# An mLSTM and a squared-ReLU feed-forward in one kernel: a new hand-written order of its 1,280 steps

## The chip, the cores and the metric

The kernel runs on one core of one Trainium2 chip. Its metric is the time of one execution on the device, in microseconds. Five engines work side by side, each through its own list of instructions in order: TensorE (PE, with its weight loads PEld), VectorE (DVE), ScalarE (ACT), GpSimd (POOL) and SyncE (SP), which here issues all DMAs. An engine waits for another by semaphores.

## The reference

The first part is a gated recurrence (mLSTM) per batch and head, with B = 4, H = 8, S = 768 and D = 40; the second is a token-shift feed-forward over the 320 joined channels, with 1,024 hidden ones.

```python
for t in range(S):
    m_new = np.maximum(f_gate[:, :, t] + m, i_gate[:, :, t])
    f_stab = np.exp(f_gate[:, :, t] + m - m_new)
    i_stab = np.exp(i_gate[:, :, t] - m_new)
    C = f_stab * C + i_stab * outer(vt, kt)
    n = f_stab * n + i_stab * kt
    h_tilde = C @ qt
    y[:, :, t] = sigmoid(o_gate[:, :, t]) * h_tilde / np.maximum(np.abs(n @ qt), 1.0)
x_prev = shift(x)                       # x is y with the heads side by side
xk = mu_k * x + (1 - mu_k) * x_prev
xr = mu_r * x + (1 - mu_r) * x_prev
k = np.maximum(xk @ w_k, 0.0)
out = sigmoid(xr @ w_r) * ((k * k) @ w_v)
```

## The kernel before

The sequence is cut into 6 chunks of 128 tokens. Two batches with the same chunk make one unit, so there are 12 units `u`, each with two halves `i`. Inside a chunk the recurrence is computed as a masked attention; between chunks a state `C` per batch is carried.

A unit's first stage goes: `load_s` brings k and q (`kq`, two loads of 320 KB, to 40 partitions each), `load_v` v and k in token order, `load_o` the output gates; `fetch_m` spreads the running maxima over all partitions and `mask` (GpSimd) makes them causal; `exps` (ScalarE) takes the exponentials; `scores` (TensorE, tile `pS`) and `weigh` (VectorE, writes `e`) give the weights; `attend` (TensorE, tiles `pI` and `pX`) the sums; `norm`, `gate`, `outcome` and `twin` scale them to `x`; `turn` (TensorE) and `turned` (ScalarE) transpose. For unit 0 there is no earlier `fetch_m`, and `spread` makes the maxima by matmuls into `pM`.

The second stage: `change` makes x minus x_prev, `mix` (VectorE, three instructions of 128x256 for each of k and r) the mixed input `xm`. fp32 products are made from parts: each operand is split into a high part (`mix_h`, ScalarE, tile `xh`) and a low part (`mix_l`, tile `xl`), and three products of parts are summed. `ffn_k` (tile `pk`), `relu`, `square`, `square_h` (`kh`) and `square_l` (`kl`) give the hidden layer in four groups, `ffn_v` (tile `pv`) the second product, `ffn_r` (tile `pr`) the gate, `result` and `store` the output.

The weights are loaded by the kernel itself as 64-bit words (`load_w`) and turned into fp32 and then into parts on the chip: `size` (ScalarE), three `bits` steps (VectorE), `parts` (ScalarE, the high part) and `parts_l` (the low part: `wkl`, `wvl`), for three of them by a `differ` on TensorE. There are 8 pieces of wk, 8 of wv and 3 of wr. `stack` copies rows of wk and wr by DMA. `warm(n)` issues n matmuls on an identity, whose result is not used.

Each engine's program is set by the list of calls at the end of the kernel: the scheduler is switched off (`manual_schedule`), and a call appends its instructions to the engines they belong to. Some calls name their engine, `V`, `G` (GpSimd), `A` or `SY` (SyncE). So the list alone decides what stands behind what on every engine and in SyncE's DMA queue. The list has 1,283 calls, from the line `every = ExitStack()` on. Semaphores order what depends on each other across engines. SyncE issues at most eight DMAs ahead: the ninth waits for the landing of the first.

Of the kernel before, what the change touches and what calls it, by code (L numbers as in the profile page):

```python
# [39 lines left out]
def mlstm_cmix_kernel(ctx: ExitStack, tc, kq, vk, og, gi, gf, wk, wr, wq, wv, mu, pad, out):  # L40
# [519 lines left out]
    load_w("wk", 0, SY)  # L560
    warm(4)
    begin()
    load_w("wk", 7, SY)
    warm(4)
    size("wk", 0)
    size("wk", 7)
    warm(4)
    load_w("wk", 6, SY)
    gate_b(0)
    warm(4)  # L570
    gate_m(0)
    load_w("wk", 2, SY)
    scale_a(0, V)
    gate_o(0, SY)
    warm(8)
    bits("wk", 0, 0)
    scale_k(0, V)
    warm(4)
    load_w("wk", 1, SY)
    load_s(0, SY)  # L580
    gate_r(0)
    gate_b(1)
    bits("wk", 0, 1)
    bits("wk", 0, 2)
    triangle()
    size("wk", 2)
    zero_state(0, G)
    size("wk", 6)
    bits("wk", 7, 0)
    load_w("wk", 5, SY)  # L590
    parts("wk", 0)
    size("wk", 1)
    bits("wk", 7, 1)
    bits("wk", 7, 2)
    bits("wk", 2, 0)
    load_w("wk", 4, SY)
    bits("wk", 1, 0)
    bits("wk", 6, 0)
    bits("wk", 2, 1)
    parts("wk", 7)  # L600
    load_w("wv", 1, SY)
    bits("wk", 1, 1)
    bits("wk", 2, 2)
    gate_i(1, V)
    zero_state(1, G)
    columns(0)
    spread(0, 0)
    exps(0, 0, 0, 4)
    load_v(0, SY)
    bits("wk", 1, 2)  # L610
    bits("wk", 6, 1)
    parts_l("wk", 0, V)
    load_o(0, SY)
    scores(0, 0)
    parts_l("wk", 7, V)
    load_w("wr", 0, SY)
    exps(0, 0, 4, 8)
    parts("wk", 2)
    bits("wk", 6, 2)
    gate_m(1)  # L620
    size("wk", 4)
    spread(0, 1)
    bits("wk", 4, 0)
    weigh(0, 0, 0)
    size("wv", 1)
    parts_l("wk", 2, V)
    bits("wk", 4, 1)
    scale_a(1, V)
    bits("wv", 1, 0)
    parts("wk", 6)  # L630
    parts("wk", 1)
    load_w("wv", 0, SY)
    gate_o(1, SY)
    scale_d(1, V)
    size("wk", 5)
    bits("wv", 1, 1)
    scale_k(1, V)
    load_w("wk", 3, SY)
    carry_in(0, 0, V)
    weigh(0, 0, 1)  # L640
    exps(0, 1, 0, 4)
    load_o(1, SY)
    gate_r(1)
    bits("wk", 5, 0)
    scores(0, 1)
    gate_b(2)
    bits("wv", 1, 2)
    bits("wk", 4, 2)
    bits("wk", 5, 1)
    gate_i(2, V)  # L650
    parts("wv", 1)
    parts("wk", 4)
    bits("wk", 5, 2)
    load_w("wr", 1, SY)
    fetch_m(1, 0, SY)
    parts_l("wv", 1, V)
    attend(0, 0)
    parts_l("wk", 1, V)
    parts("wk", 5)
    parts_l("wk", 6, V)  # L660
    warm(4)
    norm(0, 0, 0)
    norm(0, 0, 1)
    size("wv", 0)
    zero_state(2, G)
    exps(0, 1, 4, 8)
    load_s(1, SY)
    bits("wv", 0, 0)
    weigh(0, 1, 0)
    warm(4)  # L670
    size("wk", 3)
    fetch_m(1, 1, SY)
    mask(1, 0)
    warm(4)
    load_v(1, SY)
    parts_l("wk", 4, V)
    size("wr", 0)
    differ("wk", 5)
    bits("wr", 0, 0)
    warm(8)  # L680
    bits("wr", 0, 1)
    warm(4)
    norm(0, 0, 2)
    bits("wk", 3, 0)
    carry_in(0, 1, V)
    mask(1, 1)
    sigmoid_o()
    warm(4)
    load_w("wr", 2, SY)
    bits("wr", 0, 2)  # L690
    warm(4)
    bits("wv", 0, 1)
    size("wr", 1)
    parts_l("wk", 5, A)
    zero_state(3, G)
    warm(4)
    carry_add(0, 0)
    gate(0, 0, V)
    scale_a(2, V)
    outcome(0, 0, V)  # L700
    weigh(0, 1, 1)
    load_mu(SY)
    exps(1, 0, 4, 8)
    warm(4)
    bits("wr", 1, 0)
    bits("wr", 1, 1)
    bits("wv", 0, 2)
    stack("wk", 4, 4, 1, SY)
    gate_m(2)
    stack("wk", 4, 4, 0, SY)  # L710
    parts("wr", 0)
    attend(0, 1)
    bits("wk", 3, 1)
    norm(0, 1, 0)
    scores(1, 0)
    twin(0, 0, V)
    exps(1, 0, 0, 4)
    norm(0, 1, 1)
    differ("wr", 0)
    parts("wv", 0)  # L720
    bits("wk", 3, 2)
    carry_add(0, 1)
    norm(0, 1, 2)
    parts("wk", 3)
    gate(0, 1, V)
    bits("wr", 1, 2)
    turn(0, 0)
    warm(8)
    outcome(0, 1, V)
    parts_l("wr", 0, A)  # L730
    differ("wv", 0)
    twin(0, 1, A)
    turned(0, 0)
    weigh(1, 0, 0)
    weigh(1, 0, 1)
    turn(0, 1)
    parts("wr", 1)
    turned(0, 1)
    warm(4)
    parts_l("wk", 3, V)  # L740
    exps(1, 1, 0, 4)
    change(0, 0, V)
    warm(4)
    change(0, 1, V)
    carry_in(1, 0, V)
    warm(4)
    stack("wk", 0, 2, 0, SY)
    exps(1, 1, 4, 8)
    mix(0, "k")
    scores(1, 1)  # L750
    weigh(1, 1, 0)
    mix_h(0, "k")
    attend(1, 0)
    size("wr", 2)
    weigh(1, 1, 1)
    carry_in(1, 1, V)
    warm(8)
    mix_l(0, "k", V)
    bits("wr", 2, 0)
    stack("wk", 0, 2, 1, SY)  # L760
    norm(1, 0, 0)
    warm(4)
    bits("wr", 2, 1)
    norm(1, 0, 1)
    mix(0, "r")
    bits("wr", 2, 2)
    stack("wk", 2, 2, 1, SY)
    parts_l("wv", 0, A)
    norm(1, 0, 2)
    parts("wr", 2)  # L770
    columns(1)
    stack("wk", 2, 2, 0, SY)
    attend(1, 1)
    gate(1, 0, V)
    norm(1, 1, 0)
    parts_l("wr", 1, V)
    load_w("wv", 2, SY)
    outcome(1, 0, V)
    mix_h(0, "r")
    ffn_k(0, 3)  # L780
    carry_add(1, 1)
    stack("wr", 2, 1, 0, SY)
    norm(1, 1, 1)
    relu(0, 3)
    norm(1, 1, 2)
    gate_o(2, SY)
    twin(1, 0, V)
    ffn_k(0, 0)
    parts_l("wr", 2, V)
    mix_l(0, "r", V)  # L790
    stack("wr", 2, 1, 1, SY)
    relu(0, 0)
    turn(1, 0)
    load_w("wv", 3, SY)
    turned(1, 0)
    gate(1, 1, V)
    outcome(1, 1, V)
    scale_d(2, V)
    square(0, 3, A)
    size("wv", 2)  # L800
    load_w("wv", 4, SY)
    twin(1, 1, V)
    ffn_k(0, 1)
    square_h(0, 3, A)
    turn(1, 1)
# [1096 lines left out]
```

## Time and profile before

| | us |
|---|---|
| median of three runs | 332.12 (331.01 to 332.5) |
| the profiled execution's own time | 333.46 |
| its span, first to last instruction | 331.7 |
| TensorE busy / idle in the span | 317.1 / 14.6 |
| VectorE, ScalarE, GpSimd busy | 244.8, 233.1, 108.0 |
| bytes moved by DMA | 43.05 MB, mean 130 GB/s |

The profile is of one execution, whose own time lies 1.76 us over its span. "Busy" of TensorE counts pipelined matmuls; in a row of 128-column warm-ups one takes 0.26 us by its own duration, while they follow each other much faster, so paces are read from the start of one to the start of the next. The clock is the share of full speed that was granted to TensorE.

### The profile page before, as it was taken

The page shows a single profiled execution, that of the slowest core. Times are in us where ns is not written, and L with a number is a line of the kernel's source. Part 1 is how long each engine was busy: PE and PEld are TensorE (multiplying, and loading weights), DVE is VectorE, ACT ScalarE, POOL GpSimd, SP SyncE. Part 2 cuts the span into 40 slices and gives each one's busy share as a digit, 9 for nine tenths or more (in the row PEclk, how much of TensorE's full clock was granted, in tenths as well). Part 3 has the DMA queues.
Part 4 walks back from the last instruction along what each step waited for, and adds up shares of the span by engine and source line. Part 5 has one row for each costly group of instructions (what it writes and reads, how often), then busy time and mean ns, then how long its engine had stood idle before and what let it go on. Part 6 is the DMA issues. An engine that isn't in the chain of part 4 may idle for free.

```text
span 331.7 us, 8880 instructions
## 1 busy us (share of the span) xinstructions
PE 317.1 (96%) x3571; PEld 300.9 (91%) x3571; DVE 244.8 (74%) x548; ACT 233.1 (70%) x508; POOL 108.0 (33%) x128
## 2 busy tenths in 40 slices
PE   5798899989999999999999999999999999999995
PEld 4577699979989999999999999999999999999995
DVE  4698989998898794798698884797956556588111
ACT  3669858999665983936787688668749949855670
POOL 2001100122645613554513425346313157311340
PEclk9557999999999999999999999999999999999999
DMA  6989327946555253332733514536126034010001
GB/s 207 280 274 275 71 59 251 290 153 175 186 176 183 73 128 94 94 119 77 250 105 84 200 67 130 174 105 191 56 85 186 17 92 155 2 42 3 0 22 59
DMA packets 17218, 43.05 MB, mean 130 GB/s; under 512 B 4264, under 2 KB 7912, under 8 KB 16216
## 3 DMA queue, kind: packets, MB, share of 16 engines
q1 hardware_dynamic: 17176, 42.48, 42.0%
q8 instruction: 28, 0.46, 0.6%
q14 instruction: 14, 0.11, 0.1%
HBM read 37.75 MB, written 4.03 MB: 126 GB/s over the span
## 4 chain that ended last, share of the span: by engine, by line
PE 68%; DMA 9%; DVE 8%; issue 5%; ACT 5%; POOL 2%; SPq 1%; POOLq 0%; ACTq 0%
PE pk L492 24%; PE pv L547 19%; PE pI L285 6%; PE pS L255 6%; PE pr L525 6%; DMA sg<-og 4%; DMA kq<-kq 4%; PE pX L291 2%; PE pT L363 2%; ACT e L244 2%; PE pM L233 1%; POOL xlk L396 1%; DMA gi_sb<-gi 1%; PE pX L297 1%; DVE wvl L458 1%
## 5 line engine op out<-in xcount | busy, mean ns | idle before, releaser
L547 PE MATMUL pv<-wvh,kh 128*128 128x320 f32 x192 | 61.0, 317 | 0.0
L547 PE MATMUL pv<-wvl,kh 128*128 128x320 f32 x192 | 59.4, 309 | 1.2 <-DVE wvl L458 1.2
L223 POOL TENSOR_SCALAR_AFFINE_SELECT e<-e 128x1024 f32<-128x1024 f32 x22 | 25.3, 1150 | 104.3 <-DMA e<-nm 56.7
L547 PE MATMUL pv<-wvh,kl 128*128 128x320 f32 x192 | 59.1, 308 | 0.0
L492 PE MATMUL pk<-xhk,wkh 128*128 128x256 f32 x192 | 56.1, 292 | 0.0
L492 PE MATMUL pk<-xlk,wkh 128*128 128x256 f32 x192 | 54.6, 285 | 0.7 <-POOL xlk L396 0.6
L497 ACT ACTIVATE rl<-pk 128x512 f32<-128x512 f32 x48 | 28.4, 592 | 38.2 <-PE pk L492 38.1
L244 ACT ACTIVATE e<-e,acol 128x128 f32<-128x128 f32 x176 | 54.9, 389 | 0.1
L492 PE MATMUL pk<-xhk,wkl 128*128 128x256 f32 x192 | 54.3, 283 | 0.0
L518 POOL TENSOR_TENSOR kl<-kk,kh 128x512 fp32r<-128x512 f32 x21 | 28.4, 1353 | 36.3 <-DVE kh L513 20.9
L547 PEld LDWEIGHTS pv<-wvl,kh 128*128 128x128 f32 x192 | 36.1, 188 | 2.0 <-DVE wvl L458 2.0
L384 DVE SCALAR_TENSOR_TENSOR xm<-xd,mu_sb,xT 128x256 f32<-128x256 f32 x72 | 36.5, 564 | 1.8 <-POOL xd L378 1.4
L492 PEld LDWEIGHTS pk<-xlk,wkh 128*128 128x128 f32 x192 | 36.5, 190 | 1.3 <-POOL xlk L396 1.1
L492 PEld LDWEIGHTS pk<-xhk,wkh 128*128 128x128 f32 x192 | 36.5, 190 | 1.2
L260 DVE TENSOR_TENSOR e<-pS,e 128x512 f32<-128x512 f32 x48 | 32.6, 682 | 6.5 <-PE pS L255 4.0
L547 PEld LDWEIGHTS pv<-wvh,kh 128*128 128x128 f32 x192 | 36.1, 188 | 0.6
L492 PEld LDWEIGHTS pk<-xhk,wkl 128*128 128x128 f32 x192 | 36.6, 191 | 0.0
L547 PEld LDWEIGHTS pv<-wvh,kl 128*128 128x128 f32 x192 | 36.0, 187 | 0.0
L255 PE MATMUL pS<-kq 40*128 40x128 f32 x384 | 30.5, 298 | 2.3 <-DMA kq<-kq 2.3
L503 ACT ACTIVATE kk<-rl 128x512 f32<-128x512 f32 x48 | 29.9, 628 | 2.1 <-POOL kl L518 1.1
L255 PEld LDWEIGHTS pS<-kq 40*128 40x128 f32 x384 | 25.4, 198 | 6.3 <-DMA kq<-kq 2.9
L285 PE MATMUL pI<-vk_sb,e 128*64 128x41 f32 x768 | 28.2, 235 | 1.6 <-DVE e L260 1.6
(142 smaller groups left out, 723.6 us busy)
## 6 DMA issues: line engine op xcount, KB each, us to landing
e<-nm SPq DMA_DIRECT2D x22, 512.0 KB
vk_sb<-vk SPq DMA_DIRECT2D x12, 648.0 KB
kq<-kq SPq DMA_DIRECT2D x24, 320.0 KB
sg<-og SPq DMA_DIRECT2D x12, 320.0 KB
out<-sg SPq DMA_DIRECT2D x24, 160.0 KB
wst<-wk SPq DMA_DIRECT2D x8, 320.0 KB
wst<-wv SPq DMA_DIRECT2D x8, 320.0 KB
wst<-wr SPq DMA_DIRECT2D x2, 320.0 KB
```

The costliest lines, as they stand in the source:

```text
L223: G.affine_select(e, e, pattern=[[0, H], [1, L]], compare_op=ALU.is_ge, fill=NEG, base=0, channel_multiplier=-1)
L244: A.activation(e[:, h, :], src, AF.Exp, bias=acol[:, cc, b * H + h:b * H + h + 1])
L255: T.matmul(pS[j][:, p * L:(p + 1) * L], kq2[rw, 0, p, cs], kq2[rw, 1, p, cs], start=True, stop=True)
L260: V.tensor_tensor(ev, t["S", i, half], ev, op=ALU.mult)
L285: T.matmul(pI[r, at], t["e", i][:, h, r], t["va"][:, i, at], start=True, stop=True)
L384: V.scalar_tensor_tensor(xm[:, ct, :].rearrange("p (b t) -> p b t", b=NB), t["xd"][:, ct], mu_sb[:, "kr".index(nm), ct:ct + 1], xT[u % G2] ...
L492: T.matmul(pk[:, i * U:(i + 1) * U], ww, xx, start=n == 0, stop=n == len(tl) - 1)
L497: A.activation(r, t["pk", pr], AF.Relu)
L503: A.activation(kk, t["r", pr], AF.Square)
L518: eng.tensor_tensor(kl, t["kk", pr], t["kh", pr].bitcast(F32), op=ALU.subtract)
L525: T.matmul(pr[:, :DM], xx[:, i * P:(i + 1) * P], ww, start=m == 0, stop=m == len(tl) - 1)
L547: T.matmul(t["pv", i][:, :DM], xx[:, ts], ww, start=f == 0 and n == 0, stop=f == NF - 1 and n == 2)
```

## The change

Only the list of calls is written anew: the functions ahead of it are the same to the letter. The new list has 1,282 calls in another order. It holds 104 warm-up matmuls instead of 100, and `differ("wr", 0)` has gone, with `parts_l("wr", 0)` now on VectorE instead of ScalarE. 110 calls name another engine than before. By instructions: GpSimd has 13 `mix_l` instead of 6, 11 `square_l` instead of 21 and 8 `gate` instead of 12; ScalarE has 31 `square_h` instead of 27. `mix_l(u, "r")` is on GpSimd in the units 4 to 11 now (before in two of them), `mix_l(u, "k")` in five units instead of four, with unit 2's on VectorE. ScalarE loads its tables 22 times instead of 24.

The head of the list, cut:

```diff
     constants()
-    load_w("wk", 0, SY)
-    warm(4)
+    triangle()
+    load_w("wk", 2, SY)
     begin()
-    load_w("wk", 7, SY)
-    warm(4)
-    size("wk", 0)
...
     scale_a(0, V)
     gate_o(0, SY)
-    warm(8)
...
-    load_w("wk", 1, SY)
-    load_s(0, SY)
...
+    load_s(0, SY)
...
-    mix_l(2, "k", G)
+    mix_l(2, "k", V)
...
-    square_h(3, 0, V)
+    square_h(3, 0, A)
```

The first place is SyncE's queue at the start (`wst` is a loaded weight piece, `gi_sb` the input gates, `nm` the stored maxima, `kq` k and q, `vk_sb` v and k, `ar` rows of gate values):

```order
 L74 DMA gi_sb<-gi 32x768
-L416 DMA wst<-wk 128x640 x3
+L416 DMA wst<-wk 128x640 x4
 L146 DMA nm_83<-ar 32x128
-L416 DMA wst<-wk 128x640
 L186 DMA kq_74<-kq 40x2048 x2
 L416 DMA wst<-wk 128x640 x2
+L146 DMA nm_84<-ar 32x128
+L191 DMA vk_sb<-vk 128x1296
 L416 DMA wst<-wv 128x640
```

The fifth weight piece has moved ahead of the store of the maxima, and the second store of maxima ahead of v.

The second place is VectorE up to the first low part of the mixed input, `xlk`, which the first feed-forward matmul reads. Before:

```order
L378 TENSOR_TENSOR xd<-xT_80 128x3x128 x2
L266 TENSOR_TENSOR kt<-vk_sb,gk 128x320
L384 SCALAR_TENSOR_TENSOR xm<-xd,mu_sb,xT_80 128x256 x3
L260 TENSOR_TENSOR e<-pS,e 128x512 x2
L266 TENSOR_TENSOR kt<-vk_sb,gk 128x320
L396 TENSOR_TENSOR xlk<-xm,xhk 128x768
```

And in the new list:

```order
L378 TENSOR_TENSOR xd<-xT_80 128x3x128
L266 TENSOR_TENSOR kt<-vk_sb,gk 128x320
L384 SCALAR_TENSOR_TENSOR xm<-xd,mu_sb,xT_80 128x256 x6
L260 TENSOR_TENSOR e<-pS,e 128x512 x2
L396 TENSOR_TENSOR xlk<-xm,xhk 128x768
```

The mixes for r (the second three) have come in ahead of `xlk`, and the weighting `e` of the unit's last scores now stands directly before it.

The third place is TensorE from the first attention on (`pT` with `ident_71` is a warm-up, `pd` a `differ`). Before, the first warm-ups stood at the very start of the program, and the row behind the first attention began with 12 of them and the `differ` of wk 5; in the new list none stands ahead of the first attention, and 44 warm-ups come between it and that `differ`. On VectorE, at the end of the weights for the second product, the low parts `wvl` stood like this before:

```order
L458 TENSOR_TENSOR wvl<-wvf,wvh 128x320 x2
L134 SCALAR_TENSOR_TENSOR bm<-gf_sb,bm 32x128
L458 TENSOR_TENSOR wvl<-wvf,wvh 128x320
L260 TENSOR_TENSOR e<-pS,e 128x512
L266 TENSOR_TENSOR kt<-vk_sb,gk 128x320
L458 TENSOR_TENSOR wvl<-wvf,wvh 128x320
L260 TENSOR_TENSOR e<-pS,e 128x512
```

And in the new list:

```order
L458 TENSOR_TENSOR wvl<-wvf,wvh 128x320
L134 SCALAR_TENSOR_TENSOR bm<-gf_sb,bm 32x128
L458 TENSOR_TENSOR wvl<-wvf,wvh 128x320 x2
L145 TENSOR_TENSOR ar<-bm 32x128
L458 TENSOR_TENSOR wvl<-wvf,wvh 128x320
L273 TENSOR_TENSOR Cd<-C_77,dec 128x328
L273 TENSOR_TENSOR Cd<-C_76,dec 128x328
L260 TENSOR_TENSOR e<-pS,e 128x512 x2
```

The weighting of unit 2's scores has moved from between the last low parts to behind them.

More of the change, by code (lines that the diff above doesn't have):

```diff
@@ new lines, in mlstm_cmix_kernel @@
+    bits("wr", 0, 1)
+    scale_a(2, V)
+    differ("wk", 5)
+    exps(1, 0, 0, 4)
+    bits("wr", 0, 2)
+    attend(0, 1)
+    mask(1, 1)
+    parts_l("wk", 5, A)
+    scores(1, 0)
+    gate(0, 0, V)
+    gate_m(2)
+    bits("wk", 3, 2)
+    stack("wk", 4, 4, 0, SY)
+    parts("wk", 3)
+    bits("wv", 0, 2)
+    outcome(0, 0, V)
+    gate_o(2, SY)
+    warm(8)
+    norm(0, 1, 0)
+    norm(0, 1, 1)
+    norm(0, 1, 2)
+    warm(4)
+    twin(0, 0, V)
+    stack("wk", 4, 4, 1, SY)
+    exps(1, 0, 4, 8)
@@ L715, in mlstm_cmix_kernel @@
[L715 to L733, printed above, removed]
+    outcome(0, 1, V)
+    twin(0, 1, V)
+    parts("wr", 0)
+    stack("wk", 0, 2, 0, SY)
+    turned(0, 0)
+    size("wr", 1)
@@ L761, in mlstm_cmix_kernel @@
[L761 to L765 removed]
+    columns(1)
+    norm(1, 0, 1)
+    attend(1, 1)
+    norm(1, 0, 2)
+    parts_l("wv", 0, A)
+    stack("wk", 2, 2, 1, SY)
+    norm(1, 1, 0)
+    norm(1, 1, 1)
+    bits("wr", 2, 1)
+    gate(1, 0, V)
+    ffn_k(0, 3)
+    relu(0, 3)
+    parts("wr", 1)
+    norm(1, 1, 2)
+    square(0, 3, A)
+    outcome(1, 0, V)
     bits("wr", 2, 2)
[L767 to L769 removed]
@@ L1370, in mlstm_cmix_kernel @@
-    mix_h(6, "k")
-    ffn_v(5, 0, 2, 3)
-    result(5, 1)
-    scores(7, 1)
-    attend(7, 0)
+    weigh(6, 1, 1)
+    mix_h(5, "k")
+    columns(4)
+    mix_l(5, "k", V)
+    mix(5, "r")
+    ffn_k(5, 0)
+    relu(5, 0)
+    inter_v(6, 0)
+    mix_h(5, "r")
+    total(6, 0)
+    norm(6, 0, 0)
+    carry_add(6, 0)
+    ffn_k(5, 3)
+    ffn_k(5, 2)
+    exps(7, 0, 4, 8)
+    result(4, 0)
+    square(5, 0, A)
+    gate_b(5)
+    mix_l(5, "r", G)
+    norm(6, 0, 1)
+    attend(6, 1)
+    scores(7, 0)
@@ new lines, in mlstm_cmix_kernel @@
+    square_l(7, 2, V)
+    square_l(7, 3, V)
+    ffn_v(7, 1, 1, 2)
+    turned(8, 1)
+    change(8, 0, V)
+    ffn_v(7, 0, 2, 3)
+    change(8, 1, V)
+    weigh(9, 0, 0)
+    mix(8, "k")
+    ffn_v(7, 1, 2, 3)
+    ffn_v(7, 1, 3, 4)
+    fetch_m(10, 0, SY)
+    result(7, 1)
+    mix_h(8, "k")
+    ffn_v(7, 0, 3, 4)
+    scores(9, 1)
+    attend(9, 0)
+    exps(9, 1, 4, 8)
+    mix(8, "r")
+    mix_l(8, "k", G)
+    inter_v(9, 0)
+    ffn_k(8, 0)
+    load_v(11, SY)
+    total(9, 0)
+    norm(9, 0, 0)
```

1936 lines of the change are left out of this document (940 added, 996 removed).

## The prediction

> **What bounds the kernel now.** I read the page first, then its 40 slices, then stretches cut where the stages change, then who TensorE waited for, and last the chain of work and the timelines at those waits.
>
> ```profile
> span 331.7 us, 8880 instructions
> PE 317.1 (96%) x3571; PEld 300.9 (91%) x3571; DVE 244.8 (74%) x548; ACT 233.1 (70%) x508; POOL 108.0 (33%) x128
> PEclk9557999999999999999999999999999999999999
> ```
>
> TensorE is busy for 96% of the span, so an edit that moves no matmul out can win only what TensorE idles (14.6 us) or does at the half clock of slices two to four. The stretches say where that is (columns: from:to, length, busy us of PE, PEld, DVE, ACT, POOL with counts, clock, DMA share, GB/s):
>
> ```profile
> 0.00:14.70 14.70, 8.94 (x51) 7.02 (x51) 9.01 (x28) 7.40 (x21) 2.16 (x13) 0.78 0.78 222
> 14.70:26.30 11.60, 11.57 (x97) 9.73 (x98) 7.80 (x23) 6.98 (x20) 0.00 (x0) 0.50 0.87 294
> 26.30:45.30 19.00, 16.01 (x270) 13.65 (x269) 18.81 (x48) 14.88 (x36) 2.61 (x3) 0.94 0.59 154
> 45.30:74.20 28.90, 27.65 (x215) 25.97 (x213) 27.13 (x67) 25.76 (x61) 3.66 (x3) 1.00 0.64 202
> 74.20:100.00 25.80, 25.16 (x405) 23.53 (x405) 22.66 (x50) 19.49 (x47) 11.11 (x12) 1.00 0.58 175
> 100.00:200.00 100.00, 99.57 (x1144) 96.57 (x1143) 80.27 (x171) 71.30 (x153) 41.51 (x48) 1.00 0.40 122
> 200.00:300.00 100.00, 99.92 (x1193) 96.42 (x1192) 69.05 (x148) 71.91 (x148) 38.75 (x44) 1.00 0.34 102
> 328.30:331.70 3.40, 0.00 (x0) 0.00 (x0) 0.46 (x1) 0.00 (x0) 0.00 (x0) 1.00 0.17 59
> ```
>
> From 100 us on TensorE idles half a microsecond in 200: nothing is left there to win. The last 3.4 us are the final store, which both kernels end with. What can move is the start up to the first feed-forward matmul at 45.3 us, 1.25 us between 45.3 and 74.2 us, and 0.64 us before 100 us. The start is a chain, and the two later places are two waits (waits of TensorE, then the chain in order of time: start us, us, what):
>
> ```profile
> PE pS L255 <- DMA kq<-kq: 2.3, 2, 1.6
> PE pv L547 <- DVE wvl L458: 1.2, 2, 0.7
> PE pk L492 <- POOL xlk L396: 0.6, 1, 0.6
> ```
>
> ```profile
> 6.37 0.42 SPq L416
> 6.83 0.40 SPq L186
> 7.28 7.41 DMA kq<-kq
> 14.73 2.07 PE pS L255 x14
> ...
> 43.95 1.06 PE pI L285 x32
> 45.01 0.31 PE pI L297 x16
> 45.32 4.02 PE pk L492 x32
> ...
> 94.97 1.19 DVE xm L384 x3
> ...
> 96.19 0.85 ACT xhk L391
> ...
> 97.11 1.93 POOL xlk L396
> ...
> 307.66 3.84 PE pk L492 x32
> ```
>
> The first unit's k and q land at 14.7 us; from there TensorE is busy at half clock to 26.3 us, and then VectorE is (18.81 of 19.00 us) until the first unit's low part, xlk, is made:
>
> ```profile
> 26.35 0.17 DVE L334 TENSOR_SCALAR den<-pI 128x8 f32<-128x8 f32 x1 [1.77 <-PE pI L297]
> 34.70 1.36 DVE L433 SCALAR_TENSOR_TENSOR wkf<-wst,wkf 128x320 int32<-128x320 int32 x1
> 40.36 1.27 DVE L384 SCALAR_TENSOR_TENSOR xm<-xd,mu_sb,xT 128x256 f32<-128x256 f32 x3
> 43.14 0.95 DVE L396 TENSOR_TENSOR xlk<-xm,xhk 128x768 fp32r<-128x768 f32 x1
> 67.52 0.49 DVE L433 SCALAR_TENSOR_TENSOR wvf<-wst,wvf 128x320 int32<-128x320 int32 x1
> 71.90 1.37 DVE L458 TENSOR_TENSOR wvl<-wvf,wvh 128x320 fp32r<-128x320 f32 x1
> ```
>
> **The change part by part.** The same functions run with the same shapes; one difference matmul group goes (wr 0), the rest is order and, for 110 element-wise steps, the engine.
>
> *Start of the chain.* The weight load issued for 0.42 us between the first store of m and the k/q loads now stands ahead of that store. SP reaches the k/q loads 0.46 us sooner (6.37 for 6.83). The bytes ahead are the same five weight pieces, and fewer loads follow behind. The landing moves by 0 (the transfers, not the issue, set it: share 0.78) to -2 us (7.41 us is much for two loads of 320 KB, of which the second waited for others). I take -0.46, the row nearest to the cause. From the landing to the end of the first attention, TensorE's order is unchanged: 11.6 us. The 28 warm-up matmuls of the first 5 us go; they cost nothing and gave nothing, as the clock of the next 20 us shows (0.50).
>
> *VectorE up to xlk.* Adding up the paces of the rows in the new order, 1.3 us of work moves ahead of the first attention's end, into the 1.77 us of idle time in the row of 26.35: free. Behind it, 14.3 us of paces before (measured 16.8, of which the weight step of 34.70 alone took 0.9 more than its like of 67.52) become 14.9: the three mixes for r (1.27) come in, others have left. So xlk starts at 43.14 - 0.46 + 0.56 = 43.24. Before, TensorE reached the first feed-forward matmul only at 45.32, 1.2 us after xlk was there (44.09), since warm-ups and a transpose stood ahead of the last attention. Now that attention follows at once on its scores' weighting, which ends as xlk begins: 43.24 + 1.06 + 0.31 = 44.6. **Term 1: -0.7 us**, between +0.5 (k/q no earlier) and -2.2.
>
> *The wv parts.* The paces from xlk to the last low part of wv add up to 24.6 us before and 22.8 after, because the mixes for r are done already and one low part stands between fewer others. It comes 1.7 us sooner than the row of 71.90, TensorE 0.7 sooner: of 1.25 us of waiting, 0.25 stay. **Term 2: -1.0 us** (0 to -1.25).
>
> *Unit 2's xlk.* It goes from GpSimd (1.93) to VectorE (0.95), behind the mixes for r, which run beside ScalarE's 0.85. From the k mix: 0.85 + 1.93 = 2.8 before, 1.27 + 0.95 = 2.2 after. TensorE comes some 1.7 us sooner, VectorE by about as much. **Term 3: -0.3 us** (+0.5 to -0.64).
>
> *The steady state.* From the first feed-forward matmul on, TensorE's program goes 43 times instead of 46 from the small matmuls to the feed-forward ones. Such a change costs 0.18 us: 32 pk matmuls behind an attention took 4.02 us (row of 45.32), behind pv matmuls 3.84 (row of 307.66). Three of them are 0.5 us; as not every one is seen in the sum, **term 4: -0.2 us** (0 to -0.5). The engines' new shares go by these rows:
>
> ```profile
> L396 POOL TENSOR_TENSOR xlk<-xm,xhk 128x768 fp32r<-128x768 f32 x4 | 7.7, 1923 | 13.6 <-ACT xhk L391 13.6
> L518 POOL TENSOR_TENSOR kl<-kk,kh 128x512 fp32r<-128x512 f32 x21 | 28.4, 1353 | 36.3 <-DVE kh L513 20.9
> L384 DVE SCALAR_TENSOR_TENSOR xm<-xd,mu_sb,xT 128x256 f32<-128x256 f32 x72 | 36.5, 564 | 1.8 <-POOL xd L378 1.4
> L384 DVE SCALAR_TENSOR_TENSOR xm<-xd,mu_sb,xT 128x256 f32<-128x256 f32 x2 | 2.4, 1254 | 0.0
> ```
>
> GpSimd gets 7 more low parts (13 for 6, +13.4 us: six xlr, one xlk) and 10 fewer kl (11 for 21, -13.5): no load is added. ScalarE gets 4 more kh and two table loads fewer. With DVE at 70 to 80% there, all is covered as long as its lead on TensorE holds; where a step lies too late, it costs part of a microsecond, as the two waits above did. **Term 5: +0.3 us** of new waits (0 to +3).
>
> The last row above is of 97 to 99 us alone: beside GpSimd's xlk a mix takes 1.25 us instead of 0.56. The Trainium skill (SBUF — State Buffer, Who interferes with whom) states that the two engines share one port pair under an exclusive lock, so that a VectorE instruction with two SBUF inputs waits out a GpSimd one that reads SBUF. The trace agrees; by it only where GpSimd's time falls counts, and its sum is unchanged.
>
> *Sum*: -0.7 - 1.0 - 0.3 - 0.2 + 0.3 = -1.9 us on the profiled execution of 333.46 us (span 331.7 and 1.76 around it). That execution lies 1.3 us over the median of 332.12, so against the median: **330.2 us**.
>
> **The rivals.**
>
> *The clock comes later (no change).* All warm-ups before the second attention now stand in one row of 44 behind the first one. Before, the clock rose during this:
>
> ```profile
> 1.66 3.17 PE L107 MATMUL pT<-ident 128*128 128x128 bf16 x28 [1.66 <-DVE one L75]
> 26.23 1.46 PE L107 MATMUL pT<-ident 128*128 128x128 bf16 x12
> 27.49 1.34 PE L450 MATMUL pd<-wkf,ident 128*128 128x320 f32 x2
> 28.82 1.74 PE L107 MATMUL pT<-ident 128*128 128x128 bf16 x28
> ```
>
> 12 warm-ups took 0.11 us each at 26.23 and 28 took 0.06 at 28.82. At the slow pace 44 last 4.6 us, 26 to 30.5. If the clock rises only after them, the difference group, the attention and the scores behind them run at half pace. At half pace the difference takes 1.3 us (27.49 to 28.82), the attention twice 1.37, the scores 2.4 (14 took 2.07): 6.4 us, 3.2 more than at full pace, of which VectorE's queue hides about half: +1.6, and 331.8. For it: 11.6 us of small matmuls, TensorE never idle, did not raise the clock. Against it: 2.5 us of full-array matmuls did, and 44 are more than that.
>
> The Trainium skill (TensorE: Matmul & The Clock Gate, What's actually happening) has half clock until one busy window of about 3.4 us. The trace disagrees: TensorE was busy from 14.7 us and got full clock only near 28.6. By the page the clock would be up before the first attention in both kernels, and this rival would fall away.
>
> *GpSimd's longer steps come at the wrong time (slower).* Each of the 7 added low parts holds a two-input VectorE step for up to 1.9 us where a kl held it for 1.35. If TensorE waits 0.27 us at each, the gain of 1.9 is gone; from there it decides. At 0.55 us it is 3.9 against 1.9: 334.1. For it: the wait at 97 us. Against it: six of the seven are xlr, which the r matmuls alone need, several groups later, and unit 2's xlk, on which TensorE did wait, leaves GpSimd.
>
> *The start gains more (faster).* If k and q, with less queued behind them, land 2 us sooner, term 1 is -2.2 and the time 328.7. For it: 7.41 us from issue to landing. Against it: five weight pieces are still ahead, at 222 GB/s.
>
> **How the numbers follow.** Chances: forecast 0.50, clock 0.23, GpSimd 0.12, early start 0.15. A change of 0.5% (1.66 us, under 330.5 or over 333.8) is about what can be told from none. The forecast's own range is 328.8 to 331.6, two thirds of it below 330.5; with the whole early case and a trace of the clock case: faster 0.49. The clock case and the forecast's upper part make up most of "same", 0.39; GpSimd's worse half and a clock case without cover, 0.12 slower. The range over all, from the early case with term 2 in full to the middle between the clock and GpSimd cases: 327.9 to 332.7.
>
> **What would show it.** In the profile after: the k/q transfer on the chain ends near 14.2; the first feed-forward matmul starts near 44.6; TensorE's wait for wvl falls from 1.2 to about 0.3, and its wait for POOL's xlk is gone; beyond 100 us under 1 us of idle time in 200. It is wrong if the clock row is still 5 in the fifth slice, if VectorE idles before its norm steps at 26 us or more, or if new waits on xlr or kl appear among TensorE's releasers.

## The result, and the profile after

The changed kernel is slower: 335.69 us at the median of 10 runs (334.09 to 336.01 without one disturbed run) against 333.16 us for the kernel before on the same chip (331.01 to 335.09), a ratio of 1.0085 (95% interval 1.0063 to 1.0107). Run again later beside three other kernels it was 1.0121 (1.0087 to 1.0156). The forecast was 330.2 us, with 332.7 as its upper end. The profiled execution of the changed kernel took 335.52 us, 2.06 more than that of before, and its span is 2.0 us longer.

The page of the changed kernel, the rows that answer to those of before:

```profile
span 333.7 us, 8857 instructions
PE 316.2 (95%) x3572; PEld 300.7 (90%) x3572; DVE 236.1 (71%) x552; ACT 233.2 (70%) x508; POOL 104.1 (31%) x122
PEclk9999899999999999999999999999999999999999
```

TensorE is busy 0.9 us less and the span is 2.0 us longer, so it idles more: 17.5 us for 14.6. The clock row shows nothing of the slow start here, though the paces do (14 scores took 2.08 us at 13.96 us, as before); what it does show is an 8 in the fifth slice. Two of the stretches used before say where the time went (columns: from:to, length, busy us of PE, PEld, DVE, ACT, POOL with counts, clock, DMA share, GB/s):

```profile
14.70:26.30 11.60, 11.60 (x103) 9.75 (x100) 10.28 (x26) 3.79 (x10) 1.09 (x1) 1.00 0.98 332
26.30:45.30 19.00, 14.05 (x206) 11.59 (x204) 16.02 (x42) 16.46 (x42) 1.09 (x1) 0.91 0.49 132
```

In the second stretch VectorE, full before (18.81 of 19.00 us), has 3 us of holes, TensorE has 5, and the clock is 0.91. In the first, ScalarE does 3.79 us of work where it did 6.98. The waits of TensorE name who was late:

```profile
PE pT L107 <- ACT xT L370: 3.2, 2, 2.6
PE pS L255 <- DMA kq<-kq: 1.5, 2, 1.1
PE pk L492 <- DVE xlk L396: 1.4, 2, 1.1
```

ScalarE's copy of the transposed x (`turned`, L370) took the place of VectorE as what holds the start. ScalarE's timeline shows how it got late (start us, us, what, and in brackets the idle time ahead and its releaser):

```profile
21.37 0.50 ACT L422 ACTIVATE wkf<-wst 128x320 f32<-128x320 f32 x1 [1.34 <-DVE wkl L458]
22.30 0.47 ACT L444 ACTIVATE wkh<-wkf 128x320 fp32r<-128x320 f32 x1 [0.43 <-DVE wkf L433]
25.70 0.49 ACT L422 ACTIVATE wvf<-wst 128x320 f32<-128x320 f32 x1 [2.93 <-DVE wkl L458]
26.10 1.12 ACT L244 ACTIVATE e<-pM,acol 128x128 f32<-128x128 f32 x4
28.22 1.14 ACT L244 ACTIVATE e<-pM,acol 128x128 f32<-128x128 f32 x4
31.16 1.27 ACT L208 ACTIVATE sg<-sg 128x1280 f32<-128x1280 f32 x1
38.39 0.49 ACT L370 ACTIVATE xT<-pT 128x384 f32<-128x384 f32 x1
```

The `size` step of wv 0 (L422) writes one of five rotating buffers and waits 2.93 us until VectorE's low part of an earlier weight piece has been made from it. ScalarE works in order, so the exponentials of unit 0's second half, which need nothing from that step, stand behind it. In the kernel before they ran at 19.38 and 24.22 us, and the sigmoid at 27.42. Now there is no more slack: from 25.7 us on ScalarE is busy almost without a gap, and VectorE waits for it instead of the other way round:

```profile
32.46 0.49 DVE L343 TENSOR_TENSOR sg<-sg,den 128x320 f32<-128x320 f32 x1 [1.39 <-ACT sg L208]
37.60 0.49 DVE L348 TENSOR_TENSOR x<-pI,sg 128x320 f32<-128x320 f32 x1 [0.57 <-ACT C L308]
44.73 1.29 DVE L260 TENSOR_TENSOR e<-pS,e 128x512 f32<-128x512 f32 x2 [0.46 <-PE pS L255]
45.94 0.95 DVE L396 TENSOR_TENSOR xlk<-xm,xhk 128x768 fp32r<-128x768 f32 x1
```

And TensorE, which meets a hole of 2.65 us and one of 0.58 while it waits for the copies, loses its clock at 40 us: warm-ups and the difference group of wv 0 run at half pace. The first two rows are the kernel before, where that group stood ahead of the second copy and 12 warm-ups behind it; the others are the changed kernel, where 16 warm-ups and the group stand behind it.

```profile
37.08 0.81 PE L450 MATMUL pd<-wvf,ident 128*128 128x320 f32 x2 [0.57 <-ACT wrl L456]
39.36 0.83 PE L107 MATMUL pT<-ident 128*128 128x128 bf16 x12 [0.58 <-ACT xT L370]
```

```profile
35.45 0.83 PE L107 MATMUL pT<-ident 128*128 128x128 bf16 x12
38.93 0.38 PE L107 MATMUL pT<-ident 128*128 128x128 bf16 x4 [2.65 <-ACT xT L370]
40.23 1.86 PE L107 MATMUL pT<-ident 128*128 128x128 bf16 x16 [0.58 <-ACT xT L370]
41.89 1.38 PE L450 MATMUL pd<-wvf,ident 128*128 128x320 f32 x2
43.42 1.16 PE L255 MATMUL pS<-kq 40*128 40x128 f32 x16
```

The second loss is at the end, where VectorE makes the last unit's mixes and xlk beside GpSimd's low parts. In the kernel before, six mixes stood ahead of that xlk too, but no step of GpSimd ran beside them. VectorE before, then after, and GpSimd after:

```profile
303.03 2.46 DVE L384 SCALAR_TENSOR_TENSOR xm<-xd,mu_sb,xT 128x256 f32<-128x256 f32 x6
306.16 0.96 DVE L396 TENSOR_TENSOR xlk<-xm,xhk 128x768 fp32r<-128x768 f32 x1 [0.66 <-ACT xhk L391]
```

```profile
304.07 3.51 DVE L384 SCALAR_TENSOR_TENSOR xm<-xd,mu_sb,xT 128x256 f32<-128x256 f32 x6 [1.34 <-POOL xd L378]
307.50 2.05 DVE L396 TENSOR_TENSOR xlk<-xm,xhk 128x768 fp32r<-128x768 f32 x1
```

```profile
305.54 1.36 POOL L518 TENSOR_TENSOR kl<-kk,kh 128x512 fp32r<-128x512 f32 x1 [1.50 <-ACT kh L511]
307.44 1.29 POOL L518 TENSOR_TENSOR kl<-kk,kh 128x512 fp32r<-128x512 f32 x1 [0.54 <-ACT kh L511]
```

TensorE now waits 1.09 us for this xlk:

```profile
309.61 0.38 PE L492 MATMUL pk<-xlk,wkh 128*128 128x256 f32 x1 [1.09 <-DVE xlk L396]
```

To compare kernels I cut TensorE's time at four places of its timeline: the first 14 scores of unit 0 (k and q have landed), the first pk matmul of units 0, 2 and 11, and its end. By the timeline the first pk matmul starts at 45.25 us before (45.32 on the chain) and at 48.55 after.

| us on TensorE | k/q landed | landed to unit 0's pk | to unit 2's | to unit 11's | to the end |
|---|---|---|---|---|---|
| before | 14.73 | 30.52 | 52.81 | 209.44 | 20.73 |
| after | 13.96 | 34.59 | 52.20 | 207.48 | 22.07 |
| difference | -0.77 | +4.07 | -0.61 | -1.96 | +1.34 |

The sum of the last row is the 2.07 us by which TensorE ends later (330.30 for 328.23). The cuts hold nearly the same matmuls in both kernels, but not quite: five small transposes of gate rows (0.52 us) lie behind unit 2's first pk matmul before and ahead of it after. So 0.52 us of the third and fourth column changes place without being won or lost.

### The profile page after: what moved, and what is told of

Same layout as the page of the kernel before. It is cut to its first block, busy times and chain, and to the rows that moved or that the text cites. A ratio compares the mean times of both kernels' runs of the same rounds, so it can differ in the third digit from the quotient of the medians.

```text
span 333.7 us, 8857 instructions
## 1 busy us (share of the span) xinstructions
PE 316.2 (95%) x3572; PEld 300.7 (90%) x3572; DVE 236.1 (71%) x552; ACT 233.2 (70%) x508; POOL 104.1 (31%) x122
## 4 chain that ended last, share of the span: by engine, by line
PE 79%; DVE 7%; DMA 6%; ACT 4%; issue 2%; POOL 1%; SPq 1%; ACTq 0%; DVEq 0%; POOLq 0%
PE pk L492 25%; PE pv L547 23%; PE pr L525 8%; PE pS L255 7%; PE pI L285 7%; DMA kq<-kq 5%; PE pX L291 3%; PE pT L363 2%; DVE xm L384 2%; PE pX L297 1%; ACT e L244 1%; DMA gf_sb<-gf 1%; PE pT L107 1%; DVE xlk L396 1%; DVE wkl L458 1%
## 5 line engine op out<-in xcount | busy, mean ns | idle before, releaser
L223 POOL TENSOR_SCALAR_AFFINE_SELECT e<-e 128x1024 f32<-128x1024 f32 x22 | 27.1, 1230 | 91.5 <-DMA e<-nm 55.1
L497 ACT ACTIVATE rl<-pk 128x512 f32<-128x512 f32 x48 | 28.3, 594 | 38.3 <-PE pk L492 38.1
L518 DVE TENSOR_TENSOR kl<-kk,kh 128x512 fp32r<-128x512 f32 x37 | 27.8, 757 | 14.2 <-ACT kh L511 14.0
L384 DVE SCALAR_TENSOR_TENSOR xm<-xd,mu_sb,xT 128x256 f32<-128x256 f32 x72 | 35.4, 551 | 2.0 <-POOL xd L378 1.6
L255 PE MATMUL pS<-kq 40*128 40x128 f32 x384 | 31.6, 299 | 1.9 <-DMA kq<-kq 1.5
L255 PEld LDWEIGHTS pS<-kq 40*128 40x128 f32 x384 | 26.1, 198 | 6.6 <-issue 2.6
L315 DVE TENSOR_TENSOR t<-pX,gk 128x328 f32<-128x328 f32 x20 | 9.9, 497 | 27.4 <-PE pX L297 20.3
```

What stands on the lines that cost most here:

```text
L223: G.affine_select(e, e, pattern=[[0, H], [1, L]], compare_op=ALU.is_ge, fill=NEG, base=0, channel_multiplier=-1)
L255: T.matmul(pS[j][:, p * L:(p + 1) * L], kq2[rw, 0, p, cs], kq2[rw, 1, p, cs], start=True, stop=True)
L384: V.scalar_tensor_tensor(xm[:, ct, :].rearrange("p (b t) -> p b t", b=NB), t["xd"][:, ct], mu_sb[:, "kr".index(nm), ct:ct + 1], xT[u % G2] ...
L497: A.activation(r, t["pk", pr], AF.Relu)
L518: eng.tensor_tensor(kl, t["kk", pr], t["kh", pr].bitcast(F32), op=ALU.subtract)
```

## The experiments

Theory A: ScalarE's order at the start makes the 4.07 us, and the end another 1.3. Theory B: the half clock that follows makes it. Theory C: the order and the engines of the steady state are worse.

**Heads and tails exchanged.** The first kernel takes before's list up to unit 0's second pk group and after's behind it, the second the other way round.

```diff
-[after's list up to ffn_k(0, 0)]
+[before's list up to ffn_k(0, 0)]
 [what is left, in after's order]
```

> The list of before up to and with the first unit's second group of feed-forward matmuls (about 47 us), and behind it every step that is then left, in the order and on the engines of after (the difference group of wr 0 stays as in before). Theory A (the 3.3 us are lost at the start, where ScalarE's queue stands on weight steps that wait for VectorE): the first pk matmul starts at 45.3 +- 0.4 us as before and the rest keeps after's gain of about 1.2 us, so 331.5 to 332.5 us, 0.5% under before. Theory C (the loss lies in the new order and engines of the steady state): the first pk matmul at 45.3 too, but the time stays at 334.5 us or more.

Measured: 333.23 us, ratio to before 1.0019 (0.9994 to 1.0045). From the landing to the first pk matmul 29.86 us (30.52 before; as the landing came sooner too, that matmul started at 43.75 and not at 45.3); from unit 2 to unit 11 208.23; the end 22.07. The 0.5% under before did not come: between unit 0 and unit 2 the seam cost 1.2 us (54.05), with a wait of 0.91 us for unit 2's k and q and, behind it, half clock from 69.7 to 73.1 us.

> The mirror: after's list up to the second group of feed-forward matmuls, then what is left in before's order and on before's engines. Theory A: first pk matmul at 48.6 us, and the time of after or a little above it, 335.5 to 337 us. Theory C: first pk matmul at 48.6 too, but the time falls back to 331 to 333 us, since the tail is the one of before.

Measured: 338.61 us, 1.0185 (1.0156 to 1.0215). The start took 35.74 us, the end 20.74, the seam 54.57, the stretch from unit 2 to unit 11 208.54. The time lies over both expectations: against the changed kernel the start is 1.2 us longer, the seam 2.4 and the stretch to unit 11 1.1. The loss of the start goes with after's head and the loss of the end with after's tail. Theory C falls for the stretch from unit 2 to unit 11, where every kernel with after's tail took 206.9 to 208.4 us and the two with before's tail 208.54 and 209.44; it holds for the last unit alone.

**ScalarE's order, one move.**

```diff
+exps(0, 1, 0, 4)
+exps(0, 1, 4, 8)
 size("wv", 0)
...
-exps(0, 1, 0, 4)
...
-exps(0, 1, 4, 8)
```

> After, with the two steps that make the decay mask of the second half of unit 0 (exps 0,1) moved ahead of the size step of wv 0 in the list, so that on ScalarE they no longer stand behind a step that waits for a free buffer. Theory A: they run near 22.8 us instead of 26.1 and 28.2, the sigmoid starts some 2 us earlier (near 29), VectorE's 1.39 us of idle time before the gate step goes, the first unit's transposed copy comes near 36.5 instead of 38.4, TensorE's wait there falls from 2.65 to under 1.5 us and the clock holds; first pk matmul at 45.5 to 46.8, time 1.8 to 3 us under after. Theory B (the half clock at 40 us alone costs the time): as long as TensorE still waits over 2 us for the copy the gain stays under 1 us. Theory C: no gain beyond 0.5 us.

Measured: 333.70 us, 1.0059 (1.0032 to 1.0086); start 32.67 us, 1.9 less than after's 34.59. In ScalarE's timeline the masks run in the hole:

```profile
22.58 2.16 ACT L244 ACTIVATE e<-pM,acol 128x128 f32<-128x128 f32 x8
25.60 0.49 ACT L422 ACTIVATE wvf<-wst 128x320 f32<-128x320 f32 x1 [0.86 <-ACT e L244]
29.02 1.27 ACT L208 ACTIVATE sg<-sg 128x1280 f32<-128x1280 f32 x1
```

The sigmoid came 2.1 us sooner and VectorE's 1.39 us went, as theory A had it. But TensorE still waited 2.38 us for the copy, not under 1.5, and the clock fell all the same. By this execution the move is worth 1.9 us of the 4.07 with the clock still falling. The changed kernel did not run in this comparison; against its two others (1.0085 and 1.0121) the time is 0.3 or 0.6 percentage points better, 0.9 or 2 us.

**Warm-ups into the hole.** No step moves; 4 warm-ups ahead of the first `turned` become 44.

```diff
 parts("wv", 0)
-warm(4)
+warm(44)
```

> After, with 44 instead of 4 warm-up matmuls in the one place ahead of the first unit's transposed copy, so that they fill about 2.4 of the 2.65 us in which TensorE idles there. No step is moved. Theory B (the half clock at 40 to 43.3 us is what costs): the clock stays at 1.00, the 16 warm-ups behind take 1.0 instead of 1.86 us, the difference group 0.8 instead of 1.4, first pk matmul 1.2 to 1.6 us sooner (near 47.2), time 1.2 to 1.6 us under after. Theory A in its strict form (VectorE's late steps set the start, the clock costs nothing): VectorE's idle time before the second scores' weighting was 0.46 us, so at most 0.5 us. If the warm-ups delay the transposes of the second half, up to 0.3 us slower.

Measured: 334.58 us, 1.0064 (1.0033 to 1.0094); start 32.44 us, 2.15 less than after's. The clock held (1.00 from 26.3 to 45.3 us), and the 16 warm-ups and what follows them ran at full pace:

```profile
38.80 1.05 PE L107 MATMUL pT<-ident 128*128 128x128 bf16 x16 [0.58 <-ACT xT L370]
39.69 0.76 PE L450 MATMUL pd<-wvf,ident 128*128 128x320 f32 x2
40.52 1.16 PE L255 MATMUL pS<-kq 40*128 40x128 f32 x16
```

From the 16 warm-ups to the scores 1.72 us passed instead of 3.19, and to the first pk matmul 6.85 instead of 8.32: the clock is worth 1.5 us. The other 0.7 us had been won ahead of these warm-ups, and not by the edit: the `size` step of wv 0, which stands ahead of the edited place, waited 2.09 us and not 2.93, as a VectorE step ahead of it took 0.49 us where in the changed kernel it took 1.33, beside GpSimd's first `mask`. Both theories hold in part. The profiled execution (332.41 us) is near the lower end of this kernel's 332.22 to 336.78, so the stretches are read from it and not its time; the median is 0.2 or 0.6 percentage points better than the changed kernel's.

**The end, and ScalarE's order in full**, with the changed kernel beside them.

> The changed kernel once more, unedited, beside the three below on the same chip, so that their differences are not those between chips. Both theories: 0.6 to 1.1% over before; first pk matmul at 48 to 48.7 us, depending on when the first k and q land (13.2 to 13.9 us in the runs so far); TensorE from unit 11's first pk matmul to its last instruction 22.07 us (before: 20.7), with a wait of about 1.0 us for the last unit's xlk in it.

Measured: 336.94 us, 1.0121 (1.0087 to 1.0156); start 34.94 us, end 22.06.

```diff
-mix(11, "r")
 ...
 mix_l(11, "k", V)
+mix(11, "r")
```

> After, with one step moved: the three mixes for r of the last unit go behind its xlk on VectorE, as they stood at k's side only in after. Theory A+ (the end of after loses 1.3 us because xlk comes behind the r mixes, which took 1.75 us beside GpSimd's low parts): xlk starts some 1.7 us sooner, TensorE's wait of 1.04 us at 309.6 goes, unit 11's stretch on TensorE falls from 22.07 to 20.8 - 21.1 us, the time is 1.0 to 1.3 us under that of after in the same comparison. Rival: the r mixes are wanted just as early (xlr for the r matmuls of the last unit), the wait moves there: no gain.

Measured: 335.01 us, 1.0060 (1.0032 to 1.0088); the end 20.72 us, 1.34 less, just what had been lost, and no wait there. The wait of 1.33 us for GpSimd's xd ahead of the mixes stayed, so it was not the cause. In VectorE's timeline three mixes stand ahead of xlk instead of six, and xlk took 1.09 us instead of 2.05, as GpSimd's kl had mostly passed by then:

```profile
306.19 1.28 DVE L384 SCALAR_TENSOR_TENSOR xm<-xd,mu_sb,xT 128x256 f32<-128x256 f32 x3 [1.33 <-POOL xd L378]
308.67 1.09 DVE L396 TENSOR_TENSOR xlk<-xm,xhk 128x768 fp32r<-128x768 f32 x1 [1.21 <-ACT xhk L391]
309.69 2.29 DVE L384 SCALAR_TENSOR_TENSOR xm<-xd,mu_sb,xT 128x256 f32<-128x256 f32 x3
```

The next kernel has, at the start, the move of `exps(0, 1, ...)` and besides:

```diff
-exps(1, 0, 4, 8)
 carry_add(0, 1)
...
-parts("wv", 0)
-parts("wr", 0)
 turned(0, 0)
+exps(1, 0, 4, 8)
+parts("wv", 0)
+parts("wr", 0)
 size("wr", 1)
```

> After, with only ScalarE's order at the start changed: the masks of the second half of unit 0 (exps 0,1) ahead of the size step of wv 0, and ahead of the second half of unit 1's masks (exps 1,0,4,8) and of the high parts of wv 0 and wr 0 now stand the copy of the first carry (0,1) and the first transposed copy (0,0). No instruction is added, no warm-up. Theory A: VectorE's outcome step of (0,1) comes 1 us sooner than with the first move alone (34.4 for 35.5), TensorE's wait for the transposed copy falls under 1 us, so the clock stays at 1.00 up to 45 us; first pk matmul at 44.5 to 45.5 us (48.6 in after, 46.5 with the first move alone), the time 2.5 to 4 us under after, 0 to 0.5% under before. Theory B (only the clock counts): as good. Rival D (the masks of unit 1, now later, are what VectorE waits for): no more than the first move alone gave, 0.9 to 2 us under after.

Measured: 335.07 us, 1.0051 (1.0015 to 1.0087), and a start of 34.21 us: a miss. VectorE's outcome step came at 34.75 us, near the expected 34.4, but the wait for the first copy only made room for a wait of 1.91 us for the second (`exps(1, 0, 4, 8)` and the two high parts now stand ahead of it), and the clock fell at 39.8 us and stayed at half until 46.6:

```profile
38.68 1.05 PE L107 MATMUL pT<-ident 128*128 128x128 bf16 x16 [1.91 <-ACT xT L370]
40.92 2.08 PE L255 MATMUL pS<-kq 40*128 40x128 f32 x16
```

Ten of its twelve runs fall into two groups, five at 332.65 to 333.39 us with a mean clock of 0.995 and five at 335.03 to 336.69 with 0.988 to 0.990. The profile, with its 6.8 us at half clock, is of the second group.

> Both edits together: the ScalarE order of the start and the r mixes of the last unit behind its xlk. If the two losses are separate, their gains add up: first pk matmul at 44.5 to 45.5 us, unit 11's stretch 20.8 to 21.1 us, 3.5 to 5 us under after, and 0.5 to 1% under before (329 to 330.5 us where before has 332). If the lead won at the start is only waited out later, less than 3 us under after.

Measured: 333.25 us, 1.0020 (0.9994 to 1.0047), 3.7 us under after in the same comparison; start 32.03, end 20.72. The gains add up, but before is not beaten: the clock fell here too, at the start (37.7 to 41.2 us) and once more from 71.9 to 75.3 us, behind a wait for unit 2's k and q, where feed-forward matmuls take 0.47 us instead of 0.31:

```profile
70.63 1.16 PE L255 MATMUL pS<-kq 40*128 40x128 f32 x14 [1.18 <-DMA kq<-kq]
73.09 0.47 PE L547 MATMUL pv<-wvh,kl 128*128 128x320 f32 x1
```

From unit 0's pk to unit 2's it took 54.16 us, for 52.20 in the changed kernel.

**The bridge.** On the last kernel, warm-ups that write the idle bank of the difference groups, so they neither wait for the copies nor delay them.

```diff
+def warm_v(n):
+    w = bank("v", "pd")
+    for _ in range(n):
+        T.matmul(w[:, :P], ident16, ident16, start=True, stop=True)
...
 turn(0, 0)
 parts_l("wk", 3, V)
-warm(8)
-warm(4)
+warm_v(16)
...
 turn(0, 1)
+warm_v(28)
```

> The kernel with both edits (start and end), and warm-ups that write the idle PSUM bank of the difference groups, so that they neither wait for the transposed copies nor hold them up: 16 in place of 12 behind the first transposes, 28 more behind the second (1.7 us of the 1.91 us in which TensorE waits there). No other step is moved. Theory B' (with the ScalarE order mended, whether the clock falls to half at 37 to 44 us is settled by that idle time and by how the clock's window falls on it, so that runs come in two groups some 2.5 us apart): the slower group goes, clock 1.00 from 30 us on, first pk matmul at 44.5 to 45.3 us, median 1 to 1.5 us under the kernel with both edits. Rival (VectorE alone sets xlk): the first pk matmul gains at most 0.5 us. Rival E (unit 2's k and q, which land near 71 us whatever the start does, take the lead back): first pk earlier, but unit 2's first pk matmul not before 99.5 us and the median under 0.7 us better.

Measured: 329.59 us, 0.9920 (0.9896 to 0.9944); its slowest run (330.41) is faster than the fastest of before beside it (331.23). Start 30.45 us, and no kq wait at 70 us. Its page and TensorE's timeline (warm_v is L116; the lines below it are 6 higher than before):

```profile
span 328.6 us, 8923 instructions
PEclk9999999999999999999999999999999999999999
```

```profile
35.87 1.73 PE L116 MATMUL pd<-ident 128*128 128x128 bf16 x28
37.81 1.05 PE L107 MATMUL pT<-ident 128*128 128x128 bf16 x16 [0.21 <-ACT xT L376]
38.70 0.76 PE L456 MATMUL pd<-wvf,ident 128*128 128x320 f32 x2
```

It gained 1.0 percentage points on the kernel without the bridge, 3.3 us and not 1 to 1.5. The two profiled executions differ by 3.03 us: 1.58 at the start, and 1.96 between unit 0 and unit 2, where the wait of 1.18 us for k and q and the second half clock behind it are gone, less 0.5 us from there to unit 11. Those two loads were issued 1.6 us sooner than without the bridge (57.19 for 58.76 us), as the start had become shorter by as much. So rival E, by which they land near 71 us whatever the start does, does not hold: the scores made from them had ended at 69.2 us.

What sets the start shows when it is cut once more, at the warm-ups behind the second transposed copy (12 before, 16 in the others):

| us on TensorE | k/q landed to these warm-ups | from them to unit 0's pk | start |
|---|---|---|---|
| before | 24.63 | 5.89 | 30.52 |
| after | 26.27 | 8.32 | 34.59 |
| exps first | 24.22 | 8.45 | 32.67 |
| more warm-ups | 25.59 | 6.85 | 32.44 |
| ScalarE's order in full | 24.28 | 9.93 | 34.21 |
| the same and the end edit | 23.65 | 8.38 | 32.03 |
| the same and the bridge | 23.60 | 6.85 | 30.45 |

The first column was 25.59 to 26.79 us in five executions with the new list's order on ScalarE and 23.60 to 24.28 in five with a mended one; row by row the order is worth 2.0 to 2.7 us. In the second, one period of half clock is worth 1.5 us and two are 3.1; warm-ups in the hole spare them. Full clock leaves 6.85 us for before's 5.89, as the new list has the difference group of wv 0 and four more warm-ups there. So the 4.07 us are 1.64 of late copies, 0.96 of matmuls that moved behind them and 1.47 of half clock. The order alone does not secure its gain: where two periods followed, nearly all of it was lost (34.21 us; 34.13 in the next kernel, which has the same start).

**Unit 2's k and q sooner**, on the kernel with both edits.

```diff
+load_s(2, SY)
 load_w("wv", 5, SY)
...
-load_s(2, SY)
```

> The kernel with both edits, and SP issues unit 2's k and q loads ahead of the load of wv 5 (three weight loads, one gate load and one mask load sooner). Theory E (these loads take 11 us from issue at 59 us, land at 70.6 us and hold TensorE 1.2 to 1.3 us): they land by 66 us, TensorE's waits for kq behind 60 us go, and what was won at the start arrives at unit 2: from the first pk matmul to unit 2's first 52.2 to 53 us instead of 54.2; median 0.8 to 1.3 us under the kernel with both edits. Rival: the weight loads that now come later make the wv steps late instead (TensorE waits for wvl or for ScalarE's copies): no gain or up to 1 us slower.

Measured: 337.77 us, 1.0165 (1.0133 to 1.0197): a miss, and slower. The wait for kq went, but ScalarE's `size` steps of wv then stand on the weight loads that had been pushed back, and the copies of the r product (L529), which free a PSUM bank, queue behind them; ScalarE's timeline, then TensorE's:

```profile
64.17 0.48 ACT L422 ACTIVATE wvf<-wst 128x320 f32<-128x320 f32 x1 [4.79 <-DMA wst<-wv]
65.45 0.42 ACT L529 ACTIVATE sg<-pr 128x320 f32<-128x320 f32 x1
```

```profile
65.93 0.38 PE L492 MATMUL pk<-xhk,wkh 128*128 128x256 f32 x1 [3.67 <-ACT sg L529]
```

It is the loss of the start once more, at another place: a ScalarE step that waits, ahead of one that others need. From unit 0 to unit 2 it took 58.01 us instead of 54.16; the start of 34.13 us adds 2.1 more in this execution.

**Everything together**: the kernel with the bridge, that load, and the high parts of wv 0 and wr 0 behind the second `turned`.

> Both edits, the bridge of warm-ups, the early k and q loads of unit 2, and ScalarE's high parts of wv 0 and wr 0 behind the second transposed copy instead of ahead of it. If start, clock, load and end are separate losses: first pk matmul at 44.3 to 45 us, unit 2's first pk at 97 to 98 us, unit 11's stretch 20.7 us; 2 to 3 us under the kernel with both edits and 0.4 to 0.9% under before. If VectorE, busy for 18 of 19 us, holds the start: first pk not before 45.5 us and no more than 1.5 us under the kernel with both edits.

Measured: 334.86 us, 1.0078 (1.0052 to 1.0105). Start 30.23 us, end 20.72, but 57.00 from unit 0 to unit 2 (52.20 with the bridge alone): the early load again. As the start gained only 0.2, the moved high parts are worth next to nothing.

**Before's head, mended.** The first splice with the end edit and the early load.

> Before's list up to the first unit's second pk group, after's list behind it, with the end edit and the early k and q loads of unit 2. Theory (after is worse than before at the start and the end alone, and its order between unit 2 and unit 11 is 2 us better): first pk matmul at 43.7 to 45.3 us, unit 2's first pk 52.5 us later, from there to unit 11's 207.5 to 208.3 us (209.4 in before), unit 11's stretch 20.7 us; 1.5 to 2.5 us under the same splice without the two edits, and 0.3 to 0.7% under before. Rival: the gain between the units belongs to after's start too, and is lost with it: no faster than before.

Measured: 336.26 us, 1.0126 (1.0094 to 1.0158). Start 31.06, end 20.72, 207.35 from unit 2 to unit 11, and 57.54 from unit 0 to unit 2, with a wait of 3.24 us for the same copies. So the end came out as expected, the stretch to unit 11 just under its bounds, and the load spoiled the sum. The start is 1.2 us longer than in the first splice, which has the same list there: TensorE waited 2.17 us at 30.8 us, and half clock followed from 34.9 to 38.3.

## Why the prediction was wrong

*Start (term 1, -0.7).* The landing came 0.77 us sooner (forecast 0.46), the first attention took 11.6 us, and VectorE had no idle time before its norm steps, all as forecast. The step that failed is the next: "So xlk starts at 43.14 - 0.46 + 0.56 = 43.24". It adds up VectorE's paces, as if VectorE never waited. xlk started at 45.94. VectorE idled 2.81 us between 26.1 and 45.9, which is the 2.70 by which the sum was off: 2.35 for ScalarE and 0.46 for TensorE at half clock. The paces themselves were right. ScalarE's list was not gone through, although its order had changed too. The step behind it, "that attention follows at once on its scores' weighting", failed by itself. In the new list the same 12 warm-ups and transposes stand ahead of that attention as before, and the difference group and four more warm-ups have come in behind the second copy. The weighting ended at 46.0, the attention began at 47.18, and the first pk matmul at 48.55, 1.66 us after xlk was done. So TensorE's own list, counted from ScalarE's late copy on, held the start, not xlk. Instead of -0.7 the term is +3.3.

*The wv parts and unit 2's xlk (terms 2 and 3, -1.3).* The waits behaved. That for wvl is gone (1.25 us before, forecast -1.0), and a new one of 0.40 for unit 2's k and q came. The stretch came out at -0.61 as the five small transposes (0.52) moved into it. The wait for xlk lies behind unit 2's first pk matmul, as only the second one reads xlk, and so in the next stretch: 0.64 us for GpSimd's before, 0.26 for VectorE's after, -0.38 for the forecast -0.3.

*The steady state (term 4, -0.2).* Unit 2 to unit 11 took 1.96 us less:

```profile
98.06:307.50 209.44, 208.29 (x2399) 201.59 (x2396) 157.77 (x332) 149.20 (x313) 82.77 (x93) 1.00 0.36 109
100.75:308.23 207.48, 207.22 (x2391) 200.93 (x2391) 146.83 (x330) 150.89 (x317) 78.04 (x86) 1.00 0.36 113
```

TensorE's idle time fell from 1.15 to 0.26 us, by 0.89 (the xlk wait, and one of 0.43 us for VectorE's copy of x at 138.7 us, which is gone). The transposes that moved out are 0.52. What is left for the pace of the matmuls is 0.55, a little over the bounds of 0 to -0.5. Whether the counted changes from small to large matmuls make it no run shows. In four of the later executions a wait of 0.67 to 0.88 us for GpSimd's xlk of unit 4 came up in this stretch, which the term had not in it.

*New waits (term 5, +0.3, to +3).* The large one that came is worth 1.34 us, within the bounds. Its place was not named, but its mechanism was that of the GpSimd rival: two-input VectorE steps stretched by GpSimd's low parts, 3.51 us for 2.46 and 2.05 for 0.96. The Trainium skill (SBUF — State Buffer, Who interferes with whom) has it that a VectorE instruction with two SBUF inputs contends with a GpSimd instruction that reads SBUF. The end edit agrees: with the kl mostly out of the way xlk took 1.09.

*The clock rival (+1.6).* Where it was placed it did not happen in the profiled execution: the 44 warm-ups took 2.98 us, and the difference group behind them ran at full pace. In the executions of the edited kernels, where nothing ahead of them on TensorE differs, they took 3.46 to 4.36. The clock did cost 1.5 us, near the rival's 1.6, but that is luck: it came at 40 us, by a fall, not by a late rise. The forecast had asked only when the clock comes, never what could take it away again. The Trainium skill (TensorE: Matmul & The Clock Gate, Why this matters for your kernels) asks for no idle gap over about 3 us. Here less was enough, and the measurement decides: a gap of 1.91 us with one of 0.58 shortly ahead, and at unit 2's k and q one of 1.18 us in one kernel and of 0.91 in another.

## What to carry to other kernels

When a list is reordered, walk through every in-order engine that the critical engines wait for, not only the two that were busy before: a cheap step that waits for a buffer or a load holds whatever is queued behind it, and here that cost twice (2 us at the start, and 4 to 5 us behind the early load). Walk through TensorE's own list too, for what has moved behind the step it waits for. Then look for the holes that are left on TensorE before a stretch of small matmuls, and fill them with matmuls that wait for nothing, into a bank that nobody reads at that time. And when two versions differ by several losses and gains, cut TensorE's time at fixed places: the end came out at 20.72 to 20.74 or at 22.06 to 22.08 us in every kernel, where the medians blurred the same 1.34 us.

## What was not expected of the hardware

The granted clock does not come back with a busy TensorE alone. In the kernel with ScalarE's order mended it was 0.50 from 39.8 to 46.6 us although TensorE had no idle time there, and the work was mostly of 40 rows or of 64 or fewer columns:

```profile
40.00:42.00 2.00, 2.00 (x13) 1.40 (x13) 2.00 (x6) 1.39 (x5) 0.00 (x0) 0.50 0.21 50
42.00:44.00 2.00, 2.00 (x30) 1.78 (x30) 1.58 (x4) 0.42 (x1) 0.00 (x0) 0.50 0.55 166
44.00:46.00 2.00, 2.00 (x41) 1.92 (x38) 2.00 (x5) 0.53 (x2) 0.00 (x0) 0.50 0.03 8
```

In the changed kernel the half clock lasted from 39.9 to 43.3 us, half as long, and in it ran 16 full-array warm-ups and a difference group. But the kind of work does not settle it: in the second splice, with the same list there, it lasted from 38.1 to 44.9 us, and 20 such warm-ups and that group ran in it, with 1.1 us of idle time in its first half. What ends it stays open.

The clock can also be lost in full-array work by a short wait. Without the bridge it fell at 71.9 us behind 16 scores of 40 rows with a gap of 1.18 us among them, in the first splice at 69.7 us behind the same with a gap of 0.91; in the changed kernel a gap of 0.40 us there left it at 1.00. Each time it came back after 3.4 us. One list can have one such period or two: one of 3.4 us takes the mean clock of a 333 us run to 0.995, two to 0.990, as in the two groups of runs of the mended order. With the hole filled the six runs lay within 1.5 us, without it the ten within about 4.
